# Attention and mixer kernel: three blocks of two score chunks turned by a DMA transpose, the last chunk's product with v on whole tiles

## The chip, the core and the metric

The kernel runs on one core of a Trainium2 chip. The metric is device time in microseconds (us) of one execution. TensorE is called PE, VectorE DVE, ScalarE ACT, GpSimd POOL and SyncE SP, as in the profile; PEld is PE's weight load.

## What is computed

Attention with a bias made by a small network from the distance of two positions, and on its output a mixer over tokens and channels:

```python
B, H, S, D = (4, 8, 576, 64)
scores = scale * np.matmul(q, k.transpose(0, 1, 3, 2))
x = (psi_rel / psi_i)[..., None]              # log1p(|i-j|) / log1p(max(i,1))
bias = np.maximum(x @ w1 + b1, 0.0) @ w2      # 32 hidden, one value per head
scores = scores + bias.transpose(2, 0, 1)[None, :, :, :]
attn = np.exp(scores - np.max(scores, axis=-1, keepdims=True))
attn = attn / (np.sum(attn, axis=-1, keepdims=True) + 1e-09)
out = np.matmul(attn, v)
...
x = out.transpose(0, 2, 1, 3).reshape(B, S, H * D)
h = np.maximum(x.transpose(0, 2, 1) @ w_tok1, 0.0) @ w_tok2
u = x + h.transpose(0, 2, 1)
return u + np.maximum(u @ w_ch1, 0.0) @ w_ch2
```

## The kernel before

**Stages.** From 0 to about 66 us the bias is made for all 36 groups of 16 query rows and stored to device memory (`bd`). Then come 16 units, each two heads of one batch, and under their end and behind them the channel mixer (`chan1`, `chan2`) to the end of the span.

**A unit.** It has five chunks of query rows: four of 128 rows for both heads (1152 columns of scores), and a last one that holds the remaining 64 rows of both heads in one tile (640 columns). A chunk goes through these steps. `scores` (L704): products of q and k on PE into one or two `pair` banks, twelve matmuls of the shape 64*128 (64 rows of the array) in a full chunk, six of the shape 128*128 in the last. `biased` (L713, DVE): adds the bias, keeps the row maximum, writes `z`. `numer` (L726, ACT): the exponential in place in `z`. `flip` (L736, PE): transposes of 128x128 blocks of `z` into a `bank`, in groups of three, 9 blocks in a full chunk and 5 in the last. `flip_hi` (L739, ACT) and `flip_lo` (L743, DVE): the half-precision high part of the turned block and its rest, into `t2a`. `back` (L769 to L771, PE): thirty matmuls of `t2a` with the two halves of v. In the last chunk a `back` takes 64 columns of `t2a` as its weights (shape 128*64) and writes 64 partitions. After chunks 1, 3 and 4 the rows are divided by their sums (`norm`). After the unit the token mixer (`mix1`, `mix2`, lines L819 to L830) and the stores to `um` and `ul` follow.

**Beside it.** POOL makes the rests of k, q, v and x (`less`, L333), scales v (L672) and takes part in decoding the 64-bit weight words (`plain` and `halves`, L574 to L591, on DVE, POOL and ACT in turns). SP issues the bias reads (L637, L640), the raw weight reads (L314), the stores (L848, L850) and, in the channel mixer, the transposes by DMA of u (L966), four 128x128 blocks each.

**Order.** `Plan.order` sets the order of every engine when the program is built: a step has an engine, a cost, a due time from the table `DUE`, and named rooms (`Hold`) that it takes and frees, such as 5 of `z` and 9 of `t2a`. Among the steps that can start within `SLACK` the one due first is taken; on PE a step of the array shape (`mode`) in use has a bonus of `STAY`. On the chip every engine then runs its list in order, and waits on semaphores.

```python
plan = Plan({"pair": 2, "bank": 4, ..., "z": Z_BUFS, "fb": 2, "t2a": TA_BUFS, "x": X_BUFS, ...})
lead = chain("scores", add({"T": 0.9 ...}, ..., take=[*both, z], free=[gk, gq], mode=1 if c < NCH else 0))
backs.append(chain("back", add({"T": 0.917}, ..., mode=0 if c < NCH else 4)))
short_ok = add({"-": 0.0}, 0, shut_short, after=[g1_ok, *short_use])
```

The step `short_ok` stands behind the last `back`: the memory of `z` and of the bias rows then goes to the buffers `raw2`, through which the second channel weights are read twice, once for their scale and once to be decoded.

Of the kernel before, what the change touches and what calls it, by code (L numbers as in the profile page):

```python
# [10 lines left out]
F16 = mybir.dt.float16  # L11
# [16 lines left out]
NCH = 4  # L28
# [7 lines left out]
SLACK = 0.111  # L36
STAY = 31.2
# [7 lines left out]
Z_BUFS = 5  # L45
TA_BUFS = 9
X_BUFS = 2
# [3 lines left out]
ON = {'dlo': {'P': 1.78},  # L51
      'norm': {'V': (0.35, -25.45), 'A': (0.88, -10.52)},
      'over': {'A': 0.65, 'V': (0.72, 66.32)},
      'vh': {'P': (0.7, -43.07), 'V': (0.4, -1.14), 'A': (0.6, 0.34)},
      'vl': {'P': (1.36, 61.9)}}
DUE = {'blk': 14.37,
       'blkn': 0.67,
       'rect': -185.34,
       'bmm': -1.81,
       'over': -77.12,  # L60
       'put': -101.52,
       'bl': -180.52,
       'bln': 3.97,
       'sums': -54.96,
       'sumsn': 6.17,
       'measw': 137.03,
       'measwn': 4.78,
       'amax': 77.02,
       'scales': 234.45,
       'scalet': -236.81,  # L70
       'scalec': -247.84,
       'fill': 34.15,
       'fill1': 146.65,
       'tok': 32.72,
# [48 lines left out]
       'g2': 36.72,
       'ur': 176.05,
       'w2m': -21.95,
       'w2mn': 6.3}
# [123 lines left out]
def attention_mixer(ctx, tc, qT, kT, v, cst, lg, ident, wt1, wt2, wc1, wc2, out, dump=None):  # L250
# [81 lines left out]
    def less(e, o, x, y):  # L332
# [3 lines left out]
                 "kk": 1, "qq": 1, "kh": 2, "qh": 2, "tv": 1, "vs": 2, "z": Z_BUFS, "fb": 2, "t2a": TA_BUFS, "x": X_BUFS, "rc": 3,  # L336
# [20 lines left out]
    with tc.manual_schedule():  # L357
# [9 lines left out]
        st["t2a"] = [tld.tile([128, 6, 128], F16, name=f"t2a{i}") for i in range(TA_BUFS)]  # L367
# [25 lines left out]
        for i in range(Z_BUFS):  # L393
            st["z"][i] = zp.tile([128, PW], F32, name=f"z{i}")
        rect_t = [slots[:, 2, S * i:S * i + S] for i in range(8)]
        more = zp.tile([128, 8 * S], F32, name="rect")
        rect_t += [more[:, S * i:S * i + S] for i in range(8)]
# [108 lines left out]

        for x, i in late:
            if i >= GATES[0]:
                hold_back(x, (i - GATES[0]) // 2)
# [44 lines left out]
        fill0 = add({"P": 1.4}, DUE["fill"], lambda e: unit_fill(1))  # L554
        fillx = add({"P": 0.3}, DUE["fill"], lambda e: [G.memset(t, 0.0) for t in (*(x[:, 4] for x in st["x"]), *(w[:, :, S:640] for w in st["w2"]))])
# [95 lines left out]
        def unit(u):  # L651
# [4 lines left out]
            set_ok = [fill0] if u == 0 else [fill0, fill1]  # L656
# [20 lines left out]
            def high(o, ho, x, hx):  # L677
                return lambda e: copy(e, st[o][ho.i][0], st[x][hx.i])
# [469 lines left out]
```

## Time and profile before

| | us |
|---|---|
| median of 3 runs | 676.28 |
| lowest and highest of them | 673.58 and 676.59 |
| the profiled execution | 675.98 |
| its span, first to last instruction | 674.2 |

The page gives each engine's busy time over the span. The stretches of the span and the instructions by line and shape come from the trace. The granted clock is PE's, in shares of its higher level of 2.4 GHz. Matmuls are pipelined, so what a group of matmuls costs PE is read from the start of its first instruction to the start of the next group, not from the durations.

### The profile page before, as it was taken

The page shows a single profiled execution, that of the slowest core. Times are in us where ns is not written, and L with a number is a line of the kernel's source. Part 1 is how long each engine was busy: PE and PEld are TensorE (multiplying, and loading weights), DVE is VectorE, ACT ScalarE, POOL GpSimd, SP SyncE. Part 2 cuts the span into 40 slices and gives each one's busy share as a digit, 9 for nine tenths or more (in the row PEclk, how much of TensorE's full clock was granted, in tenths as well). Part 3 has the DMA queues.
Part 4 walks back from the last instruction along what each step waited for, and adds up shares of the span by engine and source line. Part 5 has one row for each costly group of instructions (what it writes and reads, how often), then busy time and mean ns, then how long its engine had stood idle before and what let it go on. Part 6 is the DMA issues. An engine that isn't in the chain of part 4 may idle for free.

```text
span 674.2 us, 17090 instructions
## 1 busy us (share of the span) xinstructions
PE 638.0 (95%) x6916; PEld 429.8 (64%) x6916; DVE 454.7 (67%) x1157; ACT 377.0 (56%) x665; POOL 236.1 (35%) x247
## 2 busy tenths in 40 slices
PE   3998898999999999999999999899999999999997
PEld 1433677888889889898988864344444444455443
DVE  5897898898999999999998875777721121022000
ACT  5899778776889879888776633455311121021000
POOL 2111758424578686765330000467720000000000
PEclk8999888999999999999999999999999999999999
DMA  8988654975443824323422189855332201210221
GB/s 325 320 298 294 217 155 164 323 259 155 147 133 100 269 89 128 103 79 109 115 60 51 35 213 312 251 164 157 110 87 86 63 1 31 63 32 1 72 69 31
DMA packets 62911, 95.58 MB, mean 142 GB/s; under 512 B 23792, under 2 KB 33264, under 8 KB 62832
## 3 DMA queue, kind: packets, MB, share of 16 engines
q1 hardware_dynamic: 53184, 73.74, 34.4%
q10 hardware_dynamic: 9648, 20.75, 10.7%
q8 instruction: 54, 0.88, 0.5%
q14 instruction: 25, 0.20, 0.1%
HBM read 69.69 MB, written 20.05 MB: 133 GB/s over the span
## 4 chain that ended last, share of the span: by engine, by line
PE 70%; DVE 11%; DMA 6%; ACT 6%; POOL 4%; issue 3%; ACTq 0%; SPq 0%; DVEq 0%; POOLq 0%
PE pair L704 8%; PE bank L736 8%; PE bank L1023 7%; PE bank L1022 7%; PE bank L1021 7%; PE bank L991 5%; PE bank L993 5%; PE bank L992 5%; PE pair L457 4%; DVE t2a L743 3%; DMA raw<-wc 3%; PE bank L769 3%; DVE z L713 3%; PE bank L771 2%; PE bank L770 2%
## 5 line engine op out<-in xcount | busy, mean ns | idle before, releaser
L743 DVE SCALAR_TENSOR_TENSOR t2a<-bank,t2a 128x384 f16<-128x384 f32 x224 | 118.4, 541 | 11.4 <-ACT t2a L739 9.2
L739 ACT ACTIVATE t2a<-bank 128x384 f16<-128x384 f32 x224 | 104.2, 478 | 36.7 <-PE bank L736 27.3
L726 ACT ACTIVATE z<-z,mx 128x576 f32<-128x576 f32 x144 | 111.2, 779 | 13.5 <-DVE mx L713 10.7
L713 DVE CUSTOM_DVE_ANT_0 z<-pair,slots 128x576 f32<-128x576 f32 x144 | 107.7, 754 | 3.4 <-PE pair L704 2.5
L736 PE MATMUL bank<-id,z 128*128 128x128 f32 x656 | 105.6, 286 | 4.3 <-DVE t2a L743 3.1
L1032 DVE SCALAR_TENSOR_TENSOR o<-bank,crow,ur 128x512 f32<-128x512 f32 x18 | 13.5, 751 | 111.1 <-PE bank L1023 111.1
L736 PEld LDWEIGHTS bank<-id,z 128*128 128x128 f32 x656 | 71.5, 142 | 17.7 <-issue 6.9
L769 PE MATMUL bank<-vh,t2a 128*128 128x65 f16 (+1 forms) x800 | 81.9, 196 | 0.1
L770 PE MATMUL bank<-vl,t2a 128*128 128x64 f16 (+1 forms) x800 | 81.5, 192 | 0.0
L771 PE MATMUL bank<-vh,t2a 128*128 128x65 f16 (+1 forms) x800 | 81.2, 193 | 0.1
L769 PEld LDWEIGHTS <-t2a 128*128 128x128 f16 (+1 forms) x800 | 74.2, 100 | 4.3 <-issue 4.0
L770 PEld LDWEIGHTS <-t2a 128*128 128x128 f16 (+1 forms) x800 | 74.3, 101 | 0.8
L771 PEld LDWEIGHTS <-t2a 128*128 128x128 f16 (+1 forms) x800 | 74.4, 100 | 0.2 <-DVE t2a L743 0.2
L991 PE MATMUL bank<-slots 128*128 128x384 f16 (+1 forms) x192 | 67.7, 353 | 0.0
L993 PE MATMUL bank<-slots 128*128 128x384 f16 (+1 forms) x192 | 67.7, 352 | 0.0
L992 PE MATMUL bank<-slots 128*128 128x384 f16 (+1 forms) x192 | 67.7, 352 | 0.0
L704 PE MATMUL pair<-kh,qh 64*128 64x288 f32 (+1 forms) x288 | 62.1, 351 | 5.8 <-DVE mx L713 5.5
L1013 ACT ACTIVATE ur<-ur,sc 128x512 f32<-128x512 f32 x18 | 13.0, 721 | 93.7 <-DMA ur<-um 79.3
L704 PE MATMUL pair<-kl,qh 64*128 64x288 f32 (+1 forms) x288 | 53.3, 302 | 0.0
L704 PE MATMUL pair<-kh,ql 64*128 64x288 f32 (+1 forms) x288 | 52.2, 297 | 0.0
L1021 PE MATMUL bank<-w2h,slots 128*128 128x512 f16 x132 | 50.0, 379 | 0.0
L1022 PE MATMUL bank<-w2l,slots 128*128 128x512 f16 x132 | 50.0, 379 | 0.0
(181 smaller groups left out, 1469.2 us busy)
## 6 DMA issues: line engine op xcount, KB each, us to landing
raw<-wc SPq DMA_DIRECT2D x48, 512.0 KB, 4.3
bd<-slots SPq DMA_DIRECT2D x36, 288.0 KB, 5.0
slots<-bd SPq DMA_DIRECT2D x16, 576.0 KB, 5.9
slots<-v SPq DMA_DIRECT2D x8, 640.0 KB, 6.8
tv<-v ACTq DMA_DIRECT2D x16, 320.0 KB, 3.2
qq<-qT ACTq DMA_DIRECT2D x16, 320.0 KB, 3.4
kk<-kT ACTq DMA_DIRECT2D x16, 320.0 KB, 3.3
um<-x SPq DMA_DIRECT2D x16, 256.0 KB, 2.5
```

The costliest lines, as they stand in the source:

```text
L704: PE.matmul(out=pairs[both[h].i][:, 512 - i + n * i:512 + n * i], lhsT=qx[x][w, c * 128:c * 128 + 128], rhs=kx[y][w, k0:k0 + i], start=(j ...
L713: V.tensor_tensor_reduce(out=st["z"][z.i][:, o], in0=pairs[ph.i][:, 512 - i:512 + i], in1=bias_m[hp][:, c, h, :] if c < NCH else bias_l[hp ...
L726: A.activation(out=zz, in_=zz, func=ACTF.Exp, bias=mx_t[z.i][:, h:h + 1], scale=-1.0)
L736: PE.transpose(banks[tb.i][:, n * 128:(n + 1) * 128], st["z"][z.i][:, 384 * i + n * 128:384 * i + (n + 1) * 128], id32)
L739: A.activation(out=st["t2a"][h.i][:, 0:m].rearrange("p n q -> p (n q)"), in_=banks[tb.i][:, 0:128 * m], func=ACTF.Copy, scale=P_SCALE)
L743: V.scalar_tensor_tensor(out=x[:, 384:384 + 128 * m], in0=banks[tb.i][:, 0:128 * m], scalar=P_SCALE, in1=x[:, 0:128 * m], op0=ALU.mult, op ...
L769: PE.matmul(out=o, lhsT=lh, rhs=vh[:, n, 0:D + 1], start=(i == 0), stop=False)
L770: PE.matmul(out=ps[q, h, 0:D], lhsT=lh, rhs=vl[:, n, :], start=False, stop=False)
L771: PE.matmul(out=o, lhsT=ll, rhs=vh[:, n, 0:D + 1], start=False, stop=(i == 4))
L991: PE.matmul(out=ps[:, 0:n], lhsT=w[0][:, c], rhs=uh[:, c], start=(c == 0), stop=False)
L992: PE.matmul(out=ps[:, 0:n], lhsT=w[0][:, c], rhs=ul[:, c], start=False, stop=False)
L993: PE.matmul(out=ps[:, 0:n], lhsT=w[1][:, c], rhs=uh[:, c], start=False, stop=(c == 3))
```

## The change

In chunks 0 and 2 of each unit (`TURNED = "10100"`) the first three of the nine blocks are no longer turned on PE. ACT writes their high part from `z` into a buffer `p` (`rest_hi`), POOL scales `z` in place and writes the rest beside it (`rest_lo`, two instructions), and one DMA transpose that SP issues turns the six half-precision blocks into `t2d` (`turn`). `back` reads these blocks from `t2d`. So 32 groups of three flips go, with their `flip_hi` and `flip_lo`.

In the last chunk `back` now takes whole 128-column weights, shifted by 64 columns where needed, so its array shape is that of the full chunks; for this `t2a` has 64 columns of zeros on either side, written once by 16 small fills on POOL (`fillt`).

`t2a` goes from 9 buffers to 8, `z` from 5 to 6, `x` from 2 to 3. Two of `t2a`, one of `z` and all of `p` and `t2d` lie in the memory of the bias rows (`more`), so scores and fills wait for the last matmul of the bias (`drawn`). The costs of some steps, `SLACK`, `STAY` and the whole table `DUE` have other numbers, so that the order moves on every engine.

```diff
-SLACK = 0.111
-STAY = 31.2
+SLACK = 0.129
+STAY = 63.41
...
-Z_BUFS = 5
-TA_BUFS = 9
-X_BUFS = 2
+Z_BUFS = 6
+TA_BUFS = 8
+TD_BUFS = 3
+P_BUFS = 3
+TURNED = "10100"
+X_BUFS = 3
...
+       'hi': -44.42,
+       'lo': -62.4,
+       'turn': -60.26,
...
-        st["t2a"] = [tld.tile([128, 6, 128], F16, name=f"t2a{i}") for i in range(TA_BUFS)]
+        st["t2a"] = [tld.tile([128, 896], F16, name=f"t2a{i}") for i in range(TA_BUFS - 2)]
...
+        st["t2a"] += [more[:, 448 * i:448 * i + 448].bitcast(F16) for i in range(2)]
+        st["p"] = [more[:, 896 + 384 * i:1280 + 384 * i].bitcast(F16) for i in range(P_BUFS)]
+        st["t2d"] = [more[:, 2048 + 384 * i:2432 + 384 * i].bitcast(F16) for i in range(TD_BUFS)]
+        st["z"][Z_BUFS - 1] = more[:, 3456:3456 + PW]
...
+        drawn = add({"-": 0.0}, 0, lambda e: None, after=mms)
...
+        fillt = add({"P": 2.0}, DUE["fill1"], lambda e: [G.memset(t[:, a:a + 64], 0.0) for t in st["t2a"] for a in (0, 832)], after=[drawn])
...
+                dma = TURNED[c] == "1"
+                if dma:
+                    p2 = Hold("p")
+
+                    def rest_hi(e, z=z, p2=p2):
+                        A.activation(out=st["p"][p2.i][:, 0:384], in_=st["z"][z.i][:, 0:384], func=ACTF.Copy, scale=P_SCALE)
+
+                    def rest_lo(e, z=z, p2=p2):
+                        o, x = st["p"][p2.i], st["z"][z.i][:, 0:384]
+                        G.tensor_scalar(out=x, in0=x, scalar1=P_SCALE, scalar2=1.0, op0=ALU.mult, op1=ALU.mult)
+                        less(e, o[:, 384:768], x, o[:, 0:384])
+
+                    def turn(e, p2=p2, h=ta[0]):
+                        SP.dma_start_transpose(out=st["t2d"][h.i].rearrange("p (n q) -> p n q", n=6), in_=st["p"][p2.i])
+
+                    s = add({"A": 0.45}, t + DUE["hi"], rest_hi, after=exps[:1], take=[p2], use=[z])
+                    s = add({"P": 1.45}, t + DUE["lo"], rest_lo, after=[s], free=[z], port=True)
+                    turned_s.append(add({"X": 1.8}, t + DUE["turn"], turn, after=[s], take=ta[:1], free=[p2]))
+                    short_use.append(turned_s[-1])
-                for i, m in enumerate(sizes):
+                for i, m in list(enumerate(sizes))[int(dma):]:
...
-                            lh, ll = th[t][:, w[h]], tl[t][:, w[h]]
-                            o = ps[q, h, 0:D + 1]
+                            d = 64 * (h - b % 2) if c == NCH else 0
+                            lh, ll = (tt[t][:, y[t] + d:y[t] + d + 128] for y in (th, tl))
+                            o = ps[:, h, 0:D + 1]
...
-                                 free=[*ta, vs], use=[hb], mode=0 if c < NCH else 4)))
+                                 free=[*ta, vs], use=[hb])))
```

Three places in the order of the two programs. On PE, the `back` of a unit's last chunk behind two groups of flips, before:

```order
L736 MATMUL bank0_66<-id32_73,z1_126 128x128 x3
L736 MATMUL bank3_69<-id32_73,z2_127 128x128 x3
L769 LDWEIGHTS t2a0_94
L769 MATMUL bank2_68<-vh0_118,t2a0_94 64x65
L770 LDWEIGHTS t2a0_94
L770 MATMUL bank2_68<-vl0_119,t2a0_94 64x64
```

and the same place now (the lines of `back` are L795 to L797, that of `flip` is L768):

```order
L768 MATMUL bank2_68<-id32_73,z2_125 128x128 x3
L768 MATMUL bank3_69<-id32_73,z2_125 128x128 x3
L795 LDWEIGHTS t2a0_95
L795 MATMUL bank1_67<-vh0_116,t2a0_95 128x65
L796 LDWEIGHTS t2a0_95
L796 MATMUL bank1_67<-vl0_117,t2a0_95 128x64
```

The output has 128 partitions instead of 64. Over the whole program the flips fall from 656 to 560, the full-chunk scores (the shape 64*128) stay at 63 runs, and the 16 entries into and 16 exits from the shape 128*64 are gone.

On POOL, about the scaling of v for the ninth unit (`tv`), before (`dm`, `slots` are weight decoding, `xl`, `ql`, `vl` rests):

```order
L333 TENSOR_TENSOR xl_91<-x1_89,xh_90 128x640
L672 TENSOR_SCALAR tv_107<-tv_107,sc_75 128x640
L576 TENSOR_SCALAR dm1_85<-raw1_83 128x512
L333 TENSOR_TENSOR ql0_113<-qq_109,qh0_112 128x640
L582 TENSOR_TENSOR dm1_85<-dc_86,ds_87 128x512
L591 TENSOR_SCALAR dm1_85<-dm1_85,sc_75 128x512
L333 TENSOR_TENSOR slots_76<-dm1_85,slots_76 128x512
L320 TENSOR_SCALAR vh0_118<-tv_107 128x10x64
L333 TENSOR_TENSOR vl0_119<-tv_107,vh0_118 128x640
```

and now, where `rect` is the memory that holds `p`:

```order
L339 TENSOR_TENSOR xl_92<-x2_90,xh_91 128x640
L753 TENSOR_SCALAR rect_128<-rect_128 128x384
L339 TENSOR_TENSOR rect_128<-rect_128 128x384
L685 TENSOR_SCALAR tv_105<-tv_105,sc_75 128x640
L589 TENSOR_SCALAR dm1_85<-raw1_83 128x512
L595 TENSOR_TENSOR dm1_85<-dc_86,ds_87 128x512
L753 TENSOR_SCALAR z1_124<-z1_124 128x384
L339 TENSOR_TENSOR rect_128<-z1_124,rect_128 128x384
L604 TENSOR_SCALAR dm1_85<-dm1_85,sc_75 128x512
L339 TENSOR_TENSOR slots_76<-dm1_85,slots_76 128x512
```

Two pairs for `rest_lo` stand between the unit's other work. The decoding of the first channel weights moves back: its first piece stands behind the ninth unit's scaling of v now, behind the seventh's before, and the last five of its twelve pieces end behind the last `rest_lo`.

On SP, about the last bias reads (L637, L640 before, L650, L653 now; `raw` are weight reads, `um` and `ul` stores), before:

```order
L637 DMA slots_76<-bd2_141 128x1152
L637 DMA slots_76<-bd3_142 128x1152
L640 DMA slots_76<-bd4_143 64x576 x2
L314 DMA raw0_82<-wc1 128x1024
L314 DMA raw1_83<-wc1 128x1024
L848 DMA um2_135<-x0_88 128x4x128
L850 DMA ul1_138<-x0_88 64x128
```

and now:

```order
L650 DMA slots_76<-bd2_139 128x1152
L650 DMA slots_76<-bd3_140 128x1152
L757 DMA_TRANSPOSE rect_128<-rect_128 128x6x128
L653 DMA slots_76<-bd4_141 64x576 x2
L320 DMA raw0_82<-wc1 128x1024
L757 DMA_TRANSPOSE rect_128<-rect_128 128x6x128
L874 DMA um2_133<-x0_88 128x4x128
L876 DMA ul1_136<-x0_88 64x128
```

The transposes stand in one list with reads that wait for a free `raw` buffer and stores that wait for a unit's end. In the order of PE a `back` of a chunk that has a `turn` stands 4.4 chunks of scores behind its own on the mean, 1 to 3 chunks behind in the ninth to fifteenth `back`, two of which have a `turn`.

## Rows read from the trace of the kernel before

**Rows 1.** The head of the page: span, and PE's busy time.

```profile
span 674.2 us, 17090 instructions
PE 638.0 (95%) x6916; PEld 429.8 (64%) x6916; DVE 454.7 (67%) x1157; ACT 377.0 (56%) x665; POOL 236.1 (35%) x247
```

**Rows 2.** Stretches: length; busy PE, PEld, DVE, ACT, POOL; granted clock, DMA share, GB/s.

```profile
62.00:126.00 64.00, 55.40 (x720) 45.37 (x710) 55.95 (x158) 49.24 (x90) 44.73 (x53) 0.92 0.65 215
126.00:180.00 54.00, 50.90 (x839) 45.33 (x838) 48.82 (x136) 40.01 (x76) 22.27 (x22) 1.00 0.67 211
180.00:392.00 212.00, 210.04 (x3395) 187.40 (x3393) 197.70 (x535) 171.28 (x319) 112.51 (x104) 1.00 0.37 106
392.00:432.00 40.00, 37.24 (x247) 20.74 (x245) 27.34 (x66) 14.25 (x25) 3.97 (x4) 1.00 0.95 289
```

**Rows 3.** Waits of PE, 62 to 392 us: total, times, longest.

```profile
PEld pair L704 <- DVE mx L713: 8.7, 15, 1.4
```

**Rows 4.** PE's timeline in the middle: start, length, line, operation, count.

```profile
257.70 0.87 PE L736 MATMUL bank<-id,z 128*128 128x128 f32 x6
258.50 0.22 PE L769 MATMUL bank<-vh,t2a 128*64 128x65 f16 x1
...
259.57 0.87 PE L736 MATMUL bank<-id,z 128*128 128x128 f32 x6
...
262.09 0.85 PE L736 MATMUL bank<-id,z 128*128 128x128 f32 x6
262.87 0.40 PE L704 MATMUL pair<-kh,qh 64*128 64x288 f32 x2
...
263.86 0.20 PE L769 MATMUL bank<-vh,t2a 128*128 128x65 f16 x1
...
264.78 0.85 PE L736 MATMUL bank<-id,z 128*128 128x128 f32 x6
265.46 0.19 PE L769 MATMUL bank<-vh,t2a 128*128 128x65 f16 x1
...
271.15 0.55 PE L736 MATMUL bank<-id,z 128*128 128x128 f32 x3
271.53 0.19 PE L769 MATMUL bank<-vh,t2a 128*128 128x65 f16 x1
```

**Rows 5.** Instructions by line and shape: busy us, mean ns, idle before them.

```profile
L743 DVE SCALAR_TENSOR_TENSOR t2a<-bank,t2a 128x384 f16<-128x384 f32 x208 | 112.2, 551 | 11.1 <-ACT t2a L739 9.2
L739 ACT ACTIVATE t2a<-bank 128x384 f16<-128x384 f32 x208 | 98.4, 486 | 34.2 <-PE bank L736 25.6 <-PE bank L771 2.4 <-issue 1.3
L587 ACT ACTIVATE slots<-dm,sc 128x512 f16<-128x512 f32 x12 | 8.5, 712 | 0.8 <-POOL dm L582 0.7
L591 POOL TENSOR_SCALAR slots<-slots,sc 128x288 f32<-128x288 f32 x4 | 2.0, 508 | 0.7 <-ACT wt2h L587 0.7
L591 POOL TENSOR_SCALAR dm<-dm,sc 128x512 f32<-128x512 f32 x24 | 17.5, 730 | 13.0 <-ACT slots L587 7.8 <-ACT w2h L587 5.2
L333 POOL TENSOR_TENSOR wt2l<-slots,wt2h 128x288 f16<-128x288 f32 x4 | 2.9, 736 | 0.3
L333 POOL TENSOR_TENSOR slots<-dm,slots 128x512 f16<-128x512 f32 x12 | 14.3, 1190 | 1.0
L645 POOL MEMSET slots<- 64x64 f32 x4 | 0.9, 226 | 0.0
```

**Rows 6.** The transposes by DMA: ns on SP's queue (min/median/max), and landing.

```profile
L966 SPq DMA_TRANSPOSE slots<-slots x14: 1190/1212/2069, 321.2 to 400.9; - x14
DMA to landing us min/median/max: 2.3/2.4/6.7
```

**Rows 7.** What SP's queue waited for: total, times, longest.

```profile
SPq L314 <- DVE dc L574: 83.3, 19, 12.0
```

**Rows 8.** Behind the units: SP's first read into `raw2`, and PE's wait for the scale.

```profile
391.73 1.38 SPq L314 DMA_DIRECT2D raw<-wc  x3
426.54 0.27 PE L292 MATMUL bank<-id,mch 128*1 128x128 f32 x1 [1.56 <-DVE mch L305]
```

More of the change, by code (lines that the diff above doesn't have):

```diff
@@ new lines @@
+ON = {'dlo': {'P': 1.9},
+      'norm': {'V': (0.35, -36.79), 'A': (0.88, 3.18)},
+      'over': {'A': 0.65, 'V': (0.72, 56.73)},
+      'vh': {'P': (0.7, -16.17), 'V': (0.4, 23.01), 'A': (0.6, -13.17)},
+      'vl': {'P': (1.36, 74.11)}}
+DUE = {'blk': 46.13,
+       'blkn': 2.08,
+       'rect': -232.71,
+       'bmm': -134.22,
+       'over': -120.58,
+       'put': -73.24,
+       'bl': -42.04,
+       'bln': 5.97,
+       'sums': -151.84,
+       'sumsn': 8.17,
+       'measw': 90.24,
+       'measwn': 4.78,
+       'amax': 104.25,
+       'scales': 323.07,
+       'scalet': -281.84,
+       'scalec': -178.66,
+       'fill': -14.62,
+       'fill1': 162.6,
+       'tok': -57.19,
+       'tokn': 3.24,
+       'dec1': 79.36,
+       'dec2': 61.91,
+       'dec3': 106.38,
+       'dec4': 116.76,
+       'dec5': -136.21,
+       'load_k': 105.83,
+       'load_q': -18.77,
+       'split_k': -79.64,
+       'split_q': 4.13,
+       'load_v': -169.03,
+       'prep_v': 43.7,
+       'prep_vh': -255.82,
+       'prep_vl': 312.44,
+       'scores': -150.45,
+       'biased': 127.67,
+       'exp': 18.59,
+       'hi': -44.42,
+       'lo': -62.4,
+       'turn': -60.26,
+       'flip': -86.15,
+       'fliphi': -282.11,
+       'flip2': 4.2,
+       'fliplo': 90.47,
+       'back': 106.94,
+       'norm': -39.66,
+       'mix0': -165.12,
+       'mix1': 14.09,
+       'relu': 5.56,
+       'mix2': -169.29,
+       'mix2b': -31.55,
+       'store': 8.59,
+       'w1': 54.35,
+       'w1n': 17.85,
+       'U0': 98.45,
+       'U0n': -0.8,
+       'U1n': -20.63,
+       'U1': 4.3,
+       'U2': 346.79,
+       'Un': 3.06,
+       'U3': 76.01,
+       'U4': 222.06,
+       'u1': 171.18,
+       'u2': 58.41,
+       'u3': 147.24,
+       'u4': 38.89,
+       'u5': 75.81,
+       'G': 366.02,
+       'G0': 89.88,
+       'G0n': 7.58,
+       'g1': 58.66,
+       'g2': 70.33,
+       'ur': 38.78,
+       'w2m': -44.97,
+       'w2mn': 7.09}
@@ L392, in attention_mixer @@
         zp = pool(short, "zp", 1)
-        for i in range(Z_BUFS):
+        for i in range(Z_BUFS - 1):
             st["z"][i] = zp.tile([128, PW], F32, name=f"z{i}")
@@ L705, in scores @@
                                           rhs=kx[y][w, k0:k0 + i], start=(j == 0), stop=(j == 2))
-                lead = chain("scores", add({"T": 0.9 if c < NCH else 0.85}, t + DUE["scores"], scores, after=[*ready, *bias_in[hp, c]],
+                lead = chain("scores", add({"T": 0.9 if c < NCH else 0.95}, t + DUE["scores"], scores, after=[*ready, *bias_in[hp, c], drawn],
                                            take=[*both, z], free=[gk, gq], use=both, mode=1 if c < NCH else 0))
@@ L729, in unit @@
                 sizes = (3, 3, 3) if c < NCH else (3, 2)
-                ta, turned_s = [Hold("t2a") for _ in sizes], []
-                for i, m in enumerate(sizes):
+                ta, turned_s = [Hold("t2d" if TURNED[c] == "1" and not i else "t2a") for i in range(len(sizes))], []
+                dma = TURNED[c] == "1"
[14 more added lines that the diff above has]
+                for i, m in list(enumerate(sizes))[int(dma):]:
                     tb, fb = Hold("bank"), Hold("fb")
```

104 lines of the change are left out of this document (12 added, 92 removed).

## The prediction

> **What bounds the kernel now.** I read the head of the page first: PE is busy for 638.0 of 674.2 us [rows 1]. A mean over stages says little, so next I cut the span into stretches [rows 2]. Between 62 and 392 us, where the units run, PE is busy for 55.40 + 50.90 + 210.04 = 316.3 of 330 us. From 180 us on it idles 2.0 of 212 us: there PE sets the pace and DVE follows (197.70 of 212). Before 180 us PE idles 8.6 + 3.1 = 11.7 us, and what it waits for there is above all DVE, which frees the score banks: 8.7 us on weight loads [rows 3]. The granted clock is 0.92 in the first 64 us and 1.00 behind them. So the units are PE-bound, with a softer stretch at the start in which DVE, POOL and ACT hold PE up a little. ACT is busy for 260.5 and POOL for 179.5 of the 330 us [rows 2].
>
> What a group costs PE can't be had from mean durations, since matmuls overlap. I read starts in the timeline [rows 4]: six flips take 265.46 - 264.78 = 0.68 us until the next `back` starts, three take 271.53 - 271.15 = 0.38.
>
> The profiled execution is 675.98 us, 1.8 over its span, and 0.3 below the median of 676.28. I make the sum against 675.98 and add the 0.3 at its end.
>
> **The change part by part.** *Flips that go.* 32 groups of three. A group that stood beside another of its kind saves 0.68 - 0.38 = 0.30 us, one that stood alone 0.38: 9.6 to 12.2 us in all. The order keeps both kinds, so I take the middle, 10.9. PE has no cover for them, so they are on the path.
>
> *The last chunk's `back`.* Its thirty matmuls in the shape 128*64 take 259.57 - 258.50 = 1.07 us, the thirty of a full chunk 264.78 - 263.86 = 0.92. The entry costs too: six flips ahead of the shape 128*64 take 0.80 us, ahead of the full shape 0.68 [rows 4]. So 16 x (0.15 + 0.12) = 4.3 us go; the lower bound is the first part alone, 2.4. The entry into full-chunk scores (262.87 - 262.09 = 0.78) is as frequent as before. PE together: 15.2 us less, between 12.0 and 16.5.
>
> *DVE and ACT.* 32 `flip_lo` of 551 ns go: 17.6 us less for DVE. On ACT 32 `flip_hi` of 486 ns give way to 32 `rest_hi`, which read 384 columns from SBUF: no such row, so between the 486 of a read from PSUM and the 712 of 512 columns from SBUF [rows 5], 0 to 7.2 us more, which the 69 us that ACT has free in the units cover. I take it at nothing. Without that cover it would cost those 7.2.
>
> *POOL.* `rest_lo` is a scaling and a subtraction of 384 columns. The rows have 288 and 512: 508 and 730 ns, 736 and 1190 ns [rows 5]. By straight lines between them 0.60 + 0.93 = 1.53 us, 49 us in all, between 40 and 61. The 16 fills cost up to 16 x 0.226 = 3.6 us. POOL goes from 179.5 to some 231 of about 315 us: it has room on the whole, but in the first 64 us it stands at 44.73 already. There the order puts 6 `rest_lo` and all fills, 9 to 13 us more, ahead of the halves of the token weights for which `mix1` waits. The order answers by running `mix1` later, with a third `x` to hold a unit. What PE loses there I can't read; the bounds are -5, where DVE's relief takes away a little over half of the 8.7 us of [rows 3], and +5, where the fills and one `rest_lo` (3.6 + 1.53) lie on the path. I take +2, nearer to the loss, since POOL's row has the least room. If PE idles longer there, the clock dip of 0.92 may widen; that lies in the +5.
>
> *SP and the turn.* A DMA transpose of four blocks holds SP's queue for 1.21 us and lands after 2.4 us, at most 6.7 [rows 6]; for six blocks 1.8 and some 3.0 by proportion. SP has the time (32 x 1.8 = 58 us). The DMA share of 0.37 in the long stretch leaves room as well. But the list is one queue: a `turn` stands behind reads that wait for a decoder to free `raw` (19 waits, 83.3 us, longest 12.0) [rows 7], and those reads and the stores stand behind the turns. Who waits for a late turn is `back`, in PE's fixed list, and everything behind it. The cover: a `back` with a turn stands 4.4 chunks behind its scores, and 80 chunks fill 330 us, 4.1 us each, so 18 us. Scores, bias and exponential of a chunk take about one chunk's time, an estimated 4.1; `rest_hi` and `rest_lo` 0.6 + 1.5, the turn 3.0. That leaves some 8.8 us for waits. I take the turns at nothing in the steady part; if a turn is later than that, the excess is PE's.
>
> The row of [rows 6] makes a block about 0.6 us of latency in a DMA, against 0.10 to 0.13 us of PE's time per flip. The Trainium skill, VectorE: DVE Perf Modes, section Rules for kernel authors, prefers TensorE for a 128x128 transpose if PSUM will do as its destination, and puts (The three transpose paths) a block at 390 ns there and 1309 ns by DMA. By its figure six blocks would be an estimated 7.9 us and the room for waits 3.9 instead of 8.8: the sum would stay, and the late turns below would cost PE 4.9 us more each. The trace does not agree on the size, so I keep to the row.
>
> *The tail.* PE's wait at 426.54 us for the scale of the second channel weights follows reads that start at 391.73, when the last `back` frees their memory [rows 8]. Those 34.8 us move with the end of the units; the list on PE between them holds 156 matmuls of `chan1` behind the last `back` in both orders. New is that the last pieces of the first channel weights are decoded only there, so that one or two of their reads stand just ahead of the 289 GB/s and 0.95 DMA share of that stretch [rows 2]. I take +0.5, bounds -1 and +3. From 432 us on nothing changes.
>
> *Sum.* -15.2 + 2 + 0.5 = -12.7: 675.98 - 12.7 + 0.3 = 663.6 us. The forecast's own range: the largest gains give 675.98 - 16.5 - 5 - 1 + 0.3 = 653.8, the smallest 675.98 - 12.0 + 5 + 3 + 0.3 = 672.3.
>
> **The rivals.** *Late turns, slower than before.* A turn that meets the longest wait of 12.0 us at SP [rows 7] is 12.0 - 8.8 = 3.2 us later than its cover, and PE stands still for that time. From five such turns the gain of 15.2 is gone and the kernel no faster; with eight of the 32, 663.6 + 8 x 3.2 = 689. For it: reads that wait stand in the same list, one landing was 6.7 us instead of 2.4 [rows 6], and two early turns have far less room. Against: the mean of those waits is 83.3 / 19 = 4.4 us, half of the room. The trace of before has no such chain, so only a chance can be given.
>
> *POOL becomes the bound early, no change.* With 44.73 + 13 = 58 us of work and the 19 us of idle that its inputs cost it before, the stretch of 64 us would take 77, 13 more: 663.6 - 2 + 13 = 675. For it: POOL's list is in order, and k, q and x of the next units come through it. Against: part of that idle was waiting for `back`s on PE, which fillers can use.
>
> *The gain is kept in the units and given back behind them.* If the late decoding of the first channel weights holds `chan1` up, the tail loses one piece's chain: 2 x (0.73 + 1.19) on POOL, 0.71 on ACT and two steps on DVE, an estimated 0.55 each after `flip_lo` [rows 5], 5.7 us: 669. Against: PE must wait for the scale at the end of that stretch in any case, so a shorter hold is hidden.
>
> **How the numbers follow.** Forecast 663.6 with 0.64; given back behind the units, 669, 0.11; POOL early, 675, 0.12; late turns, 689, 0.13. A measurement of this kernel tells about 0.5%, 3.4 us, from no change, so "faster" is below 672.9: 0.64 + 0.11 = 0.75. Same 0.12, slower 0.13. The range goes from 654 to 677: below the forecast's own lower end lies little, and above 677 the late turns.
>
> **What would show it.** Right: PE's flips 560; no shape 128*64; PE's busy time from 62 us to the end of the units down by about 15 us and its idle there within 3 us of 13.7; the read into `raw2` at 378 to 381 instead of 391.73; DVE's idle in the middle up; no group of waits of `back` on the DMA above 3 us in total. Wrong: waits of the weight loads of `back` for `t2d` or the DMA, PE's idle before 126 us above 14 us with POOL above 58 of 64, or more than 40 us between the first read into `raw2` and the scale. A granted clock below 0.9 in a stretch behind 126 us would mean that PE waits there.

## The result

The changed kernel takes 659.52 us (median of 4 runs, 657.92 to 660.83), the kernel before 676.43 beside it (4 runs, 673.58 to 678.52): ratio 0.9752, 95% interval 0.9708 to 0.9795. Forecast were 663.6 and a range of 654 to 677, so the direction and the range held and the gain was 4 us larger than the forecast. The profiled execution took 660.83 us.

In the changed kernel the scores stand at L717, the flips at L768, `flip_hi` and `flip_lo` at L771 and L774, `back` at L795 to L797, `rest_hi` at L749, `rest_lo` at L753 and L339, the turn at L757 and the raw weight reads at L320.

The head of the page after, which answers to [rows 1]:

```profile
span 659.0 us, 16970 instructions
PE 624.8 (95%) x6820; PEld 421.6 (64%) x6820; DVE 439.1 (67%) x1125; ACT 373.7 (57%) x665; POOL 285.0 (43%) x328
```

The span is 15.2 us shorter. PE has 13.2 us less work, DVE 15.6 less and POOL 48.9 more. The stretches after, cut at the end of the units, which answer to [rows 2] (length; busy PE, PEld, DVE, ACT, POOL; granted clock, DMA share, GB/s):

```profile
62.00:126.00 64.00, 53.63 (x698) 42.95 (x690) 51.19 (x152) 45.59 (x84) 41.46 (x64) 0.89 0.63 163
126.00:180.00 54.00, 52.67 (x858) 48.02 (x859) 47.87 (x127) 44.69 (x86) 37.70 (x45) 1.00 0.99 256
180.00:377.00 197.00, 195.83 (x3302) 177.37 (x3303) 185.71 (x521) 164.30 (x310) 135.47 (x138) 1.00 0.58 151
377.00:417.00 40.00, 39.73 (x263) 22.24 (x260) 32.09 (x82) 18.36 (x32) 15.76 (x17) 1.00 1.03 307
```

From 62 us to the end of the units PE is busy 302.1 of 315 us, where it was 316.3 of 330: 14.2 us of work less, and 12.9 us idle against 13.7. In the 40 us behind the units it idles 0.3 instead of 2.8. What PE's weight loads waited for from 62 to 377 us (total, times, longest; compare [rows 3]):

```profile
PEld pair L717 <- DVE mx L726: 10.8, 21, 1.6
PEld bank L768 <- ACT z L739: 3.1, 5, 1.8
PEld bank L768 <- DVE t2a L774: 2.9, 13, 0.6
```

The whole list holds no wait for a DMA, so none for a turn. The moved steps by line and shape (busy, mean ns, idle before), which answer to [rows 5]; the flips from the buffers in the bias rows' memory are the 91 that read `rect`, and of the 32 `rest_hi` and `rest_lo` the rows show the 26 whose `z` lies outside that memory:

```profile
L768 PE MATMUL bank<-id,z 128*128 128x128 f32 x469 | 76.9, 289 | 3.2 <-ACT z L739 2.0 <-DVE t2a L774 0.5 <-DVE x L868 0.4
L768 PE MATMUL bank<-id,rect 128*128 128x128 f32 x91 | 14.6, 281 | 1.1 <-ACT rect L739 1.1
L749 ACT ACTIVATE rect<-z 128x384 f16<-128x384 f32 x26 | 13.6, 521 | 0.3
L753 POOL TENSOR_SCALAR z<-z 128x384 f32<-128x384 f32 x26 | 14.0, 538 | 21.7 <-ACT rect L749 21.5
L339 POOL TENSOR_TENSOR rect<-z,rect 128x384 f16<-128x384 f32 x26 | 23.9, 920 | 2.2
```

The turns (ns on SP's queue, landing; compare [rows 6]), and what SP's queue waited for (compare [rows 7]):

```profile
L757 SPq DMA_TRANSPOSE rect<-rect x32: 1212/1230/2220, 77.2 to 357.8; - x32
DMA to landing us min/median/max: 2.7/2.8/8.7
```

```profile
SPq L757 <- ACT rect L749: 52.0, 16, 7.3
SPq L757 <- POOL rect L339: 33.7, 18, 2.7
SPq L320 <- DVE dc L587: 13.2, 12, 2.8
```

Six blocks hold the queue no longer than four did, 1.23 us. The queue now stands 52.0 + 33.7 = 86 us in front of turns whose halves aren't made yet; the waits of weight reads for DVE's decoding step fell from 83.3 to 13.2 us. Behind the units (compare [rows 8]), from the timeline of SP and of PE:

```profile
377.13 2.63 SPq L320 DMA_DIRECT2D raw<-wc  x3
```

```profile
409.64 0.27 PE L298 MATMUL bank<-id,mch 128*1 128x128 f32 x1
```

The units end 14.6 us earlier, and PE makes the scale's matmul 32.5 us later without a wait, where it had been 34.8 us and 1.56 us of waiting.

The pace of the units themselves can be read from a step that DVE makes once in each, the addition of the token mixer to `x`. These are the fourth and the fourteenth of them, before and after:

```profile
176.65 0.75 DVE L842 SCALAR_TENSOR_TENSOR x<-bank,sc,x 128x512 f32<-128x512 f32 x1
364.55 0.74 DVE L842 SCALAR_TENSOR_TENSOR x<-bank,sc,x 128x512 f32<-128x512 f32 x1
```

```profile
174.14 0.75 DVE L868 SCALAR_TENSOR_TENSOR x<-bank,sc,x 128x512 f32<-128x512 f32 x1
351.96 0.74 DVE L868 SCALAR_TENSOR_TENSOR x<-bank,sc,x 128x512 f32<-128x512 f32 x1
```

Ten units of the middle take 177.8 us instead of 187.9: 10.1 us of the gain lie there, 2.5 before them.

### The profile page after: what moved, and what is told of

It is laid out like the page before. It is cut to its first block, busy times and chain, and to the rows that moved or that the text cites. A ratio compares the mean times of both kernels' runs of the same rounds, so it can differ in the third digit from the quotient of the medians.

```text
span 659.0 us, 16970 instructions
## 1 busy us (share of the span) xinstructions
PE 624.8 (95%) x6820; PEld 421.6 (64%) x6820; DVE 439.1 (67%) x1125; ACT 373.7 (57%) x665; POOL 285.0 (43%) x328
## 3 DMA queue, kind: packets, MB, share of 16 engines
q10 hardware_dynamic: 9648, 20.75, 10.7%
## 4 chain that ended last, share of the span: by engine, by line
PE 73%; DVE 9%; DMA 7%; ACT 7%; POOL 2%; issue 2%; SPq 0%; ACTq 0%; DVEq 0%; POOLq 0%
PE pair L717 8%; PE bank L768 7%; PE bank L1048 7%; PE bank L1049 7%; PE bank L1047 7%; PE bank L1017 6%; PE bank L1018 6%; PE bank L1019 6%; PE pair L468 4%; DMA raw<-wc 4%; PE bank L795 2%; PE bank L797 2%; PE bank L796 2%; DVE t2a L774 2%; DVE z L726 2%
## 5 line engine op out<-in xcount | busy, mean ns | idle before, releaser
L739 ACT ACTIVATE z<-z,mx 128x576 f32<-128x576 f32 (+1 forms) x120 | 92.5, 779 | 15.6 <-DVE mx L726 14.2
L726 DVE CUSTOM_DVE_ANT_0 z<-pair,slots 128x576 f32<-128x576 f32 (+1 forms) x120 | 89.6, 756 | 6.1 <-PE pair L717 3.0
L774 DVE SCALAR_TENSOR_TENSOR t2a<-bank,t2a 128x384 f16<-128x384 f32 (+1 forms) x150 | 79.8, 536 | 11.5 <-ACT t2a L771 10.0
L771 ACT ACTIVATE t2a<-bank 128x384 f16<-128x384 f32 (+1 forms) x150 | 70.3, 474 | 24.2 <-PE bank L768 18.9
L768 PE MATMUL bank<-id,z 128*128 128x128 f32 x469 | 76.9, 289 | 3.2 <-ACT z L739 2.0
L717 PE MATMUL pair<-kh,qh 64*128 64x288 f32 (+1 forms) x288 | 62.4, 352 | 6.8 <-DVE mx L726 6.3
L768 PEld LDWEIGHTS bank<-id,z 128*128 128x128 f32 x469 | 52.3, 145 | 12.4 <-issue 4.5
L795 PE MATMUL bank<-vh,t2a 128*128 128x65 f16 x558 | 59.7, 196 | 0.0
L796 PE MATMUL bank<-vl,t2a 128*128 128x64 f16 x558 | 59.5, 192 | 0.0
L797 PE MATMUL bank<-vh,t2a 128*128 128x65 f16 x558 | 59.4, 194 | 0.0
L717 PE MATMUL pair<-kl,qh 64*128 64x288 f32 (+1 forms) x288 | 52.8, 303 | 0.0
L796 PEld LDWEIGHTS <-t2a 128*128 128x128 f16 x558 | 51.8, 99 | 0.6
L795 PEld LDWEIGHTS <-t2a 128*128 128x128 f16 x558 | 51.6, 97 | 0.5 <-issue 0.2
L797 PEld LDWEIGHTS <-t2a 128*128 128x128 f16 x558 | 51.6, 97 | 0.0
L717 PE MATMUL pair<-kh,ql 64*128 64x288 f32 (+1 forms) x288 | 51.6, 297 | 0.0
```

What stands on the lines that cost most here:

```text
L717: PE.matmul(out=pairs[both[h].i][:, 512 - i + n * i:512 + n * i], lhsT=qx[x][w, c * 128:c * 128 + 128], rhs=kx[y][w, k0:k0 + i], start=(j ...
L726: V.tensor_tensor_reduce(out=st["z"][z.i][:, o], in0=pairs[ph.i][:, 512 - i:512 + i], in1=bias_m[hp][:, c, h, :] if c < NCH else bias_l[hp ...
L768: PE.transpose(banks[tb.i][:, n * 128:(n + 1) * 128], st["z"][z.i][:, 384 * i + n * 128:384 * i + (n + 1) * 128], id32)
L774: V.scalar_tensor_tensor(out=block(h.i, 3, m), in0=banks[tb.i][:, 0:128 * m], scalar=P_SCALE, in1=block(h.i, 0, m), op0=ALU.mult, op1=ALU. ...
L795: PE.matmul(out=o, lhsT=lh, rhs=vh[:, n, 0:D + 1], start=(i == 0), stop=False)
L796: PE.matmul(out=ps[:, h, 0:D], lhsT=lh, rhs=vl[:, n, :], start=False, stop=False)
```

## The experiments

All ratios are to runs of the kernel before on the same chip and in the same session (medians 674.0 to 674.6). The first session ran the changed kernel again.

**The changed kernel again.**

> The changed kernel again, on the same chip as the three runs beside it. Expected 658 to 661 us, 2.3 to 2.7% below the kernel before; PE's wait for the scale behind the units none or below 1 us, where the kernel before has 2.8 us of idle there. If the missing wait was chance, some 2 to 3 us of it come back here.

Measured: 658.21 us, ratio 0.976 (0.9733 to 0.9787). PE waits 0.2 us for the scale, so the missing wait wasn't chance. The differences below are from this run; it was not made again in the two later sessions, on other chips, and there the differences go by the ratios.

**The shape of the last chunk's `back`.** The old 64-column weights, in the new order:

```diff
-d = 64 * (h - b % 2) if c == NCH else 0
-lh, ll = (tt[t][:, y[t] + d:y[t] + d + 128] for y in (th, tl))
+d, m = (64 * h, 64) if c == NCH else (0, 128)
+lh, ll = (tt[t][:, y[t] + d:y[t] + d + m] for y in (th, tl))
```

> The changed kernel with the last chunk's products with v in the old shape (64 columns of weights, 64 partitions out); every engine's order is that of the changed kernel. My theory: PE is bound in the units and each of the 16 groups costs 0.15 us more inside and up to 0.12 at its entry, so 2.4 to 4.3 us slower than the changed kernel, 662 to 664 us. The rival, that PE's time in the units is hidden behind DVE: no difference, 659 to 660.

Measured: 660.98 us, ratio 0.9801 (0.9773 to 0.983): 2.8 us more, a little below the 662 to 664 us that I had put. The intervals of the two overlap, so this rests on the medians. The profiled execution, the shortest of its five, took 658.0 us, less than the 658.97 of the changed kernel's; in it ten units of the middle take 179.0 us, and 177.9 in the changed kernel run again. The sign is likely, the size is open.

**Less work in the old order.** Three kernels take from the kernel before, in 28 of the 32 groups, what the turning takes away: PE's flips, DVE's `flip_lo`, and both. Every list keeps its order, ACT still makes its `flip_hi`, and where the flips are out the banks are read with a scale of 1e-6, which the lines below don't show.

```diff
-for n in range(m):
+for n in range(0 if u > 1 and c in (0, 2) and i == 0 else m):   # flips out
     PE.transpose(banks[tb.i]...)
...
+if u > 1 and c in (0, 2) and i == 0:                            # flip_lo out
+    return
 V.scalar_tensor_tensor(...)
```

> The kernel before, with TensorE's three transposes left out of the first group of chunks 0 and 2 from the third unit on: 28 groups of 3 of the 32 that the change takes off TensorE. Every instruction of the other engines stays, in the same order (ScalarE and VectorE still read the bank), so the output is not the reference's in those blocks; the whole reading of the groups' banks is scaled down so that it stays finite. Theory (TensorE bounds the middle of the kernel, a group of three costs 0.34 us of its path): 28 x 0.34 = 9.5 us less, 662 to 667 us beside 674. Rival (VectorE sets the pace, its work being unchanged here): no more than 2 us less, 672 or above.

> The kernel before, with VectorE's subtraction (flip_lo) left out of the same 28 groups; TensorE, ScalarE and the order are as before, and the output is not the reference's. It takes 28 x 0.54 = 15 us off VectorE. Theory (TensorE bounds the middle): 0 to 3 us less, 671 to 674. Rival (VectorE sets the pace): 8 us less or more, 666 or below.

> The kernel before, with both TensorE's three transposes and VectorE's subtraction left out of the same 28 groups (chunks 0 and 2 from the third unit on); ScalarE's half stays and the order is as before, so the output is not the reference's in those blocks. That is what the turned chunks take off the two engines. Theory (the two hold each other up: each alone left the time within 2 us, since the other stayed at 94 to 98% of the middle stretch): 7 to 10 us less, 664 to 667 beside 674. Rival (something else sets the pace, ScalarE or the order of steps; the changed kernel's gain comes from its order): within 3 us of before, 671 or above.

Measured: without the flips 675.96 us, ratio 1.0017 (0.9998 to 1.0037); without `flip_lo` 673.34, ratio 0.998 (0.9962 to 0.9998); without both 673.91, ratio 0.9987 (0.9968 to 1.0006). By the medians none is worth more than 1.3 us, by the intervals none more than 2.6. The stretch from 180 to 374 us (columns as above) of the kernel before:

```profile
180.00:374.00 194.00, 192.04 (x3116) 172.15 (x3113) 184.27 (x498) 162.00 (x302) 111.11 (x103) 1.00 0.37 110
```

Without the flips, and what PE's weight loads waited for there (this wait was 2.7 us in 12 times before):

```profile
180.00:374.00 194.00, 187.46 (x3041) 165.97 (x3038) 182.49 (x497) 160.03 (x300) 110.51 (x102) 1.00 0.37 110
```

```profile
PEld bank L736 <- DVE t2a L743: 6.8, 16, 2.2
```

Without `flip_lo`:

```profile
180.00:374.00 194.00, 192.03 (x3142) 172.50 (x3141) 176.97 (x479) 161.35 (x302) 111.01 (x102) 1.00 0.36 110
```

Without both, and the same wait of the weight loads:

```profile
180.00:374.00 194.00, 188.48 (x3010) 167.56 (x3009) 173.91 (x470) 158.47 (x298) 110.48 (x102) 0.97 0.36 110
```

```profile
PEld bank L736 <- DVE t2a L745: 6.2, 14, 1.7
```

With the flips out, PE is idle 6.5 us of the stretch instead of 2.0, and waits longer for the `bank` that an earlier `flip_lo` frees. With both out PE idles 5.5, DVE 20.1 and ACT 35.5 us: no engine is full, and the end doesn't come earlier. The clock plays into the row of both: PE idled 2.7 us from 220 to 240 us, and from 240 to 260 us its granted clock was 0.82 (1.00 before), which put the units of this execution some 3.5 us back. It isn't the answer, though: the five executions of this kernel with a mean granted clock of 0.986 or 0.987, that of the kernel before, took 671.6 to 674.1 us, at most 3 us less than before, where 7 to 10 were expected. The first kernel by itself came out as DVE as the bound would have it, the second as PE would, and the third as neither. So both readings fell that I had held, PE alone as the bound and PE with DVE. In the old lists the freed time stays lying between the instructions.

**The same work put back in the new order.** In the changed kernel the second group of chunks 0 and 2 is flipped twice on PE, or has its `flip_lo` made twice on DVE:

```diff
-for n in range(m):
+for n in [*range(m)] * (2 if TURNED[c] == "1" and i == 1 else 1):   # PE, flips twice
...
+for _ in range(2 if TURNED[c] == "1" and i == 1 else 1):            # DVE, flip_lo twice
     V.scalar_tensor_tensor(...)
```

> The changed kernel, where TensorE makes the three transposes of the second group of chunks 0 and 2 twice (32 groups of 3 more, what the turning had taken away, 0.33 us each, 10.7 us); order and all else unchanged. Theory (in the changed kernel TensorE is the bound of the middle, 99% busy): 7 to 11 us over the changed kernel, ratio to before 0.987 to 0.993. Rival (VectorE or the reads set the pace, TensorE has that much to spare): less than 4 us, ratio 0.982 or below.

> The changed kernel, where VectorE makes the subtraction of the second group of chunks 0 and 2 twice (32 more, 0.54 us each, 17 us: what the turning had taken away); order and all else unchanged. VectorE was idle 10.6 us of the 194 from 180 to 374, where about 22 of the 32 lie (12 us). Theory (two engines share the pace): 4 to 12 us over the changed kernel, ratio to before 0.983 to 0.995. Rival (TensorE alone bounds, VectorE's idle time covers it): less than 3 us, ratio 0.981 or below.

Measured: PE's part 665.88 us, ratio 0.9862 (0.9832 to 0.9892), 6.9 us more for 10.7 us of work; DVE's part 672.0 us, ratio 0.9955 (0.9936 to 0.9974), 13 us more for 17.6 us of work. PE's part lies just under the 7 to 11 us expected if PE bounds, DVE's a little over the 4 to 12 expected of a shared pace: work put back on either costs time, so neither bounds alone. The second round also holds its bank longer, which these runs don't part from the work. The page's chain that ended last, by engine, shows who carries it. Kernel before:

```profile
PE 70%; DVE 11%; DMA 6%; ACT 6%; POOL 4%; issue 3%; ACTq 0%; SPq 0%; DVEq 0%; POOLq 0%
```

The kernel before without flips and `flip_lo`:

```profile
PE 62%; DVE 15%; ACT 7%; DMA 6%; POOL 4%; issue 4%; SPq 1%; ACTq 0%; DVEq 0%; POOLq 0%
```

The changed kernel, then with the flips twice, then with `flip_lo` twice:

```profile
PE 73%; DVE 9%; DMA 7%; ACT 7%; POOL 2%; issue 2%; SPq 0%; ACTq 0%; DVEq 0%; POOLq 0%
```

```profile
PE 82%; DVE 6%; DMA 5%; ACT 4%; issue 1%; POOL 0%; SPq 0%; ACTq 0%; DVEq 0%
```

```profile
PE 62%; DVE 25%; ACT 5%; DMA 4%; issue 3%; POOL 1%; SPq 0%; ACTq 0%; DVEq 0%; POOLq 0%
```

More work on PE lets the chain run on PE, more on DVE moves it to DVE, and less on both leaves it hopping: PE's share falls from 70 to 62%, and DVE's rises from 11 to 15%.

**The new numbers without the turning.**

```diff
-TURNED = "10100"
+TURNED = "00000"
```

> The changed code with no chunk turned by DMA: the new due times, buffers, the products of the last chunk on whole tiles and the bias rows' memory stay, the flips go back to TensorE, and the planner lays the order out anew. Theory (the turned chunks bring some 11 us, the rest of the change the 2.8 us that the last chunk's shape was measured at, and little else): 668 to 673 us. Rival (the order that the new numbers give is what brought the gain, not the turning): 657 to 662 us.

Measured: 683.53 us, ratio 1.0125 (1.0095 to 1.0155), 9 us slower than the kernel before; neither expectation held. It has the shape of the last chunk's `back`, the due times, the sixth `z` and the third `x` of the changed kernel, and 8 of `t2a` where the kernel before had 9. Its first stretch:

```profile
62.00:126.00 64.00, 52.18 (x583) 40.85 (x576) 51.00 (x138) 42.50 (x77) 35.36 (x57) 0.81 0.49 161
```

PE gets 583 matmuls done there instead of 698, at a mean granted clock of 0.81 instead of 0.89. The order's numbers bring nothing by themselves. That they were made for lists without those groups is a likely reason, but which part of them costs the 9 us isn't shown.

The traces tell where it is lost. Ten units of the middle, read as above in each profiled execution:

| kernel | fourth unit, us | fourteenth, us | between |
|---|---|---|---|
| before | 176.65 | 364.55 | 187.90 |
| before, without the flips | 176.35 | 365.14 | 188.79 |
| before, without `flip_lo` | 176.07 | 363.55 | 187.48 |
| before, without both | 175.75 | 366.75 | 191.00 |
| new numbers, no turning | 184.08 | 372.91 | 188.83 |
| changed, again | 171.83 | 349.71 | 177.88 |
| changed, flips twice | 175.78 | 357.83 | 182.05 |
| changed, `flip_lo` twice | 173.85 | 361.39 | 187.54 |

Without the turning the new lists keep the old pace in the middle, and 7.4 of the 9 us are lost before it. (The start is the less steady part: two executions of the changed kernel reach the fourth unit at 174.14 and 171.83 us and take 177.8 and 177.9 for the ten.) In the new lists `flip_lo` put back takes 9.7 of the 10.0 us gained there, for 11.0 us of DVE's work; the flips put back take 4.2, for 6.6 of PE's.

**A late turn.** Every turn issued twice, the second waiting for the first:

```diff
+for _ in range(2):
     SP.dma_start_transpose(out=st["t2d"][h.i]..., in_=st["p"][p2.i])
```

> The changed kernel with every turn issued twice: the second transpose writes the same blocks again, so SP issues 64 instead of 32, and a turn is complete some 1.5 to 3 us later. My theory: a back with a turn has some 8.8 us of room, so within 1.5 us of the changed kernel. The rival, late turns: each of the 32 backs waits 1.5 to 3 us longer, 15 us or more slower in all if only a third of them has no room, 670 us and above.

Measured: 692.95 us, ratio 1.0284 (1.024 to 1.0327), 35 us more than the changed kernel, where I had put at most 1.5. `back` hardly waits for the turned blocks: its longest group of waits on that DMA is 3.8 us in total. The time goes through SP's queue. What it waited for second turns in all; then its timeline, DVE's and PE's around the largest waits:

```profile
SPq L758 <- DMA rect<-rect: 77.5, 32, 7.3
```

```profile
196.02 1.22 SPq L758 DMA_TRANSPOSE rect<-rect  x1
197.35 8.66 SPq L320 DMA_DIRECT2D raw<-wc  x3
```

```profile
204.97 0.69 DVE L314 TENSOR_REDUCE m<-raw 128x1 f32<-128x512 f32 x1 [6.05 <-DMA raw<-wc]
205.57 0.55 DVE L775 SCALAR_TENSOR_TENSOR t2a<-bank,t2a 128x384 f16<-128x384 f32 x1
```

```profile
206.17 0.90 PE L769 MATMUL bank<-id,z 128*128 128x128 f32 x3 [4.96 <-DVE t2a L775]
```

Weight reads are issued behind the second turn, from 197.35 us on, and land some 7 us later, where their median is 4.4 in the changed kernel; the third of the row waits 6.6 us for that. DVE stands 6.05 us in front of the maximum of those weights; the `flip_lo` that frees PE's bank stands behind it in DVE's list; and PE waits 4.96 us. Such a wait costs more than its length: from 206 to 212 us, behind it, PE's granted clock is 0.54, near its lower level of 1.2 GHz, and from 180 to 260 us it is 0.91, where the changed kernel has 1.00.

**The queue held, the turn on time.** Behind each turn two small reads into one unused tile, the second waiting for the first:

```diff
 SP.dma_start_transpose(out=st["t2d"][h.i]..., in_=st["p"][p2.i])
+for _ in range(2):
+    SP.dma_start(out=held, in_=ident[:, 0:32])
```

> The changed kernel, where each of the 32 turns is issued once, and behind it SyncE issues two small reads (16 KB) into one unused tile, the second of which waits for the first. So the turned blocks land when they did, but SyncE's queue is held some 3 us longer per turn, near to what the doubled turn held it (1.2 us of issue and 2.4 of waiting). Theory A (the doubled turn cost its 35 us because what stands behind it on SyncE's queue, the weights' and the bias rows' reads, came late, and VectorE and ScalarE wait for those in their order): 20 to 35 us over the changed kernel, 680 to 694. Theory B (it cost that because the turned blocks came late for the products with v): within 5 us of the changed kernel, 657 to 664.

Measured: 683.44 us, ratio 1.0118 (1.0091 to 1.0145), 24 us over the changed kernel by the ratios: theory A. From 62 to 374 us SP's queue waited 81.0 us for those reads, where it had waited 72.8 for the second turns, and DVE again for weights and for bias rows, 0.6 and 2.4 us in the changed kernel:

```profile
SPq L760 <- DMA held<-ident: 81.0, 31, 9.5
```

```profile
DVE m L314 <- DMA raw<-wc: 8.2, 4, 5.6
DVE z L727 <- DMA slots<-bd: 4.4, 1, 4.4
```

No `back` waits for a DMA, and the granted clock from 180 to 260 us is 0.90 here too. It isn't wholly clean: two waits, of 7.1 us on ACT and 8.6 on POOL, are put down to the small reads themselves, though neither engine uses their tile.

**A slower POOL.** The subtraction of `rest_lo` made twice, some 30 us more on POOL:

```diff
 less(e, o[:, 384:768], x, o[:, 0:384])
+less(e, o[:, 384:768], x, o[:, 0:384])
```

> The changed kernel with the subtraction of each rest on GpSimd made twice, 32 x 0.9 = 30 us more work there. If GpSimd has room in the units (about 213 of 312 us busy), the middle hides it and only the first stretch with its 6 rests and little room shows it: 1 to 6 us slower. If GpSimd were the bound of the first stretch already, all of 6 x 0.9 = 5.4 us there and more behind: 6 to 15 us slower. If it has room everywhere: within 1 us.

Measured: 667.37 us, ratio 0.9914 (0.9888 to 0.994), 9 us more. Ten units of the middle take 184.1 us, 6.2 more, so most of it lies there, where I had expected POOL's room to hide it. Part of it may be DVE: its integer steps of the weight decoding take longer beside the doubled subtraction. They are in the changed kernel, then with the doubled subtraction:

```profile
L592 DVE SCALAR_TENSOR_TENSOR dc<-dm,dc 128x512 int32<-128x512 int32 x27 | 20.2, 750 | 1.8 <-POOL dm L589 1.6
L587 DVE TENSOR_SCALAR dc<-raw 128x512 int32<-128x512 int32 x27 | 15.7, 582 | 7.3 <-POOL dm L595 6.1 <-DMA raw<-wt 1.0
```

```profile
L592 DVE SCALAR_TENSOR_TENSOR dc<-dm,dc 128x512 int32<-128x512 int32 x27 | 22.4, 829 | 1.8 <-POOL dm L589 1.6
L587 DVE TENSOR_SCALAR dc<-raw 128x512 int32<-128x512 int32 x27 | 19.4, 718 | 6.2 <-POOL dm L595 6.1
```

That is 5.9 us on DVE; at the price of the doubled `flip_lo` (13 us for 17.6) an estimated 4.4 of the 9. What the rest is isn't shown.

**The reads behind the units.** The fifth of the first twelve reads of the second channel weights issued three times:

```diff
-load_words(e, st[raw.kind][raw.i], w2_in[f], 512)
+for _ in range(3 if f == 4 and first_pass else 1):
+    load_words(e, st[raw.kind][raw.i], w2_in[f], 512)
```

> The changed kernel, where the fifth of the first twelve reads of the last weights is issued three times, each waiting for the one before, so that the reads behind it and the scale made from their maxima come some 5 us later; order and all else unchanged. Theory (in the changed kernel the scale comes just when TensorE needs it, because its reads stand ahead of the token transposes on SyncE's queue; before, TensorE waited 2.76 us for it): TensorE waits 2 to 5 us for the scale, 2 to 5 us over the changed kernel, ratio to before 0.979 to 0.984. Rival (there is cover, and the tail's gain lies elsewhere): less than 1 us, no wait for the scale.

Measured: 664.87 us, ratio 0.9857 (0.9828 to 0.9885), 6.5 us over the changed kernel by the ratios. The wait isn't where I expected it. SP's timeline at the repeated read, PE's wait and PE's scale:

```profile
380.87 8.23 SPq L320 DMA_DIRECT2D raw<-wc  x3
```

```profile
393.76 0.32 PE L1017 MATMUL bank<-slots 128*128 128x384 f16 x1 [3.85 <-DVE x L868]
412.28 0.27 PE L298 MATMUL bank<-id,mch 128*1 128x128 f32 x1
```

```profile
392.36 0.69 DVE L314 TENSOR_REDUCE mch<-raw 128x1 f32<-128x512 f32 x1 [5.67 <-DMA raw<-wc]
392.96 0.74 DVE L868 SCALAR_TENSOR_TENSOR x<-bank,sc,x 128x512 f32<-128x512 f32 x1
```

The scale comes without a wait. DVE, whose rows are the last two, stood 5.67 us for a read, with the last unit's `x` (L868) behind it, and PE waited 3.85 us for that. So reads there are on the path through DVE's list, not through the scale. The profiled execution is 4.1 us over the changed kernel's (span 661.3 against 657.2), and the wait covers nearly all of that; the other 3 us of the difference between the medians I can't place.

## Why the prediction came right, and where it didn't

*The flips that go (10.9 us) and PE as the bound.* This step failed in its reason. I took PE's 210.04 of 212 us for proof that work taken off PE is time. With the flips taken out in place the time is the same within 0.4%, and so it is when `flip_lo` goes too. Put back in the new order, PE's part costs 6.9 us and DVE's 13, and the two aren't a sum, since the gain is 16. DVE's gain, which I had counted at nothing beyond the early stretch, is at least as dear as PE's, and in the middle dearer: 9.7 of the 10.0 us gained there go again when it is put back, 4.2 with PE's. The sign that I had named, more idle time on DVE in the middle, didn't appear: 11.3 of 197 us, as against 14.3 of 212 [rows 2]. The changed kernel fills both engines as full as before, and is done sooner. So the total came out near for a reason that the prediction doesn't give: less work on both engines, and lists laid anew around it. Neither brought anything alone in the kernels tried (0.9987 and 1.0125). That flips counted at their full price stood near to what the two brought together is in part luck.

What in the old lists keeps the time isn't settled. The kernels with work taken out left two things as they were, the order and the rooms: each emptied group still takes a `bank`, one of two flip rooms (`fb`) and a `t2a`, and ACT still reads it. That PE waits for `flip_lo` to free a bank, 6.2 us even with both parts out, speaks for the rooms; it wasn't tried apart. Nor was an order of its own tried for the old work, so how much of the gain better numbers alone could bring is open.

*The last chunk's `back` (4.3, at least 2.4).* Not contradicted: 2.8 by the medians, with intervals that overlap. The 1.1 us in ten units of the middle would be an estimated 1.7 for all 16, below my lower bound, so the 4.3 was likely too much.

*The early stretch (+2).* Mis-sized, and better: PE idles 11.7 us from 62 to 180, the same as before (of the 8.7 us of [rows 3], which I had read as lying there, 1.2 come later), and POOL stands at 41.46 of 64, not 58. The new work came where I had counted it: 6 `rest_lo` and the 16 fills lie between 62 and 126 us. The fills took 1.5 us, not 3.6, and I hadn't taken off the old work that the order moves out of this stretch, from 44.73 to some 31 us; from 126 to 180 us POOL rises from 22.27 to 37.70. So the rival of a POOL-bound start fell.

*Turns at nothing, 8.8 us of room.* The row came out (no wait of `back` on a DMA), the reason didn't. I looked at `back` as the one that waits for a late turn; it is what stands behind the turn on SP's queue, and behind the late read on DVE's. Of the sizes, ACT's `rest_hi` (521 ns, between my 486 and 712) and POOL's 0.54 + 0.92 us (I had 0.60 + 0.93) held; a turn of six blocks takes 1.23 us on the queue, not 1.8, and lands after 2.8, not 3.0. The Trainium skill, VectorE: DVE Perf Modes, section The three transpose paths, gives 1309 ns for one block by DMA; as a price per block the trace doesn't agree, with 2.8 us for six, 0.47 each.

*The rival of late turns.* It didn't happen, but it was nearer than its price showed: some 3 us more of SP's queue per turn makes the kernel slower than before (1.0118 and 1.0284), and not by the wait of `back` that I had priced.

*The tail (+0.5).* Mis-sized: 281.9 us from the first read into `raw2` to the end, where it was 282.5, so -0.6. PE's idle there fell by 2.5 us. In the old list of SP three transposes stood between the third and the fourth of the reads, which were issued from 391.73 and at 402.22 us; in the new one the fourth to sixth read stand ahead of the next transposes, and the fourth is issued 4.7 us after the first, not 10.5. That this order brings the 2.5 us is read from the traces and not shown by a run.

*The sum.* By the two profiled executions the units end 14.6 us earlier, where 15.2 - 2 = 13.2 were forecast, and the part behind them is 0.6 shorter, where it was to be 0.5 longer: 15.2 us in place of 12.7. The medians of the two kernels lie 16.9 apart. The read into `raw2` comes at 377.13 us, just ahead of the 378 to 381 that I had named.

## What to carry to other kernels

An engine that is 99% busy in a kernel with fixed lists need not be what alone bounds it: take its work out in place first, and if the time stays, as it did here, look for the gain in lists and buffers laid anew around the freed time, and ask again which engine is dearest there. When a transfer is added to an in-order queue, ask first what stands behind it there and which engine stops in order for that, and only then who uses what it brings.

## What the runs showed of the hardware

- A DMA transpose of six 128x128 half-precision blocks holds SP's queue as long as one of four (1.23 against 1.21 us) and lands little later (2.8 against 2.4).
- 72.8 to 81.0 us more of waiting on SP's queue between 62 and 374 us, in some 30 pieces, came with 24 to 35 us more of the whole; the dearer of the two kernels, the one with 72.8, also issued 32 more transposes of 1.2 us each.
- Behind a wait of 4.96 us PE's granted clock was 0.54 from 206 to 212 us. Shorter gaps didn't always show: with 2.7 us of idle from 220 to 240 us the next 20 us had 0.82 in one kernel, with 3.3 us 1.00 in another (both parts out, and the flips alone).
- DVE's integer steps slowed from 582 to 718 ns and from 750 to 829 when POOL's subtractions were doubled, 30 us more of work, while its pass over the scores, which reads PSUM too, stayed at 748 and 747. The Trainium skill, SBUF — State Buffer, section Terms, has the two engines share a pair of ports that one of them holds for a whole instruction; the rows agree with it. POOL's busy time alone doesn't set the size: in the kernel before, with 48.9 us less on POOL than the changed kernel has, the first of the two steps took 621 ns.
